# Score matmuls in row tiles: two batches issued one behind the other, with four buffers for the transposed Q and K

## The chip, the cores and the metric

The kernel runs on one core of a Trainium2 chip. The metric is the device time of one execution in microseconds (us). Every number is of executions that were not slow, except where a slow one is the subject. The time before was 304.8 us (median of 3 runs).

The names of the engines: PE is TensorE's matmuls, PEld its weight loads, DVE VectorE, ACT ScalarE, POOL GpSimd, SPq the queue that issues transfers. "L300" is line 300 of the kernel.

## The reference, cut to what matters

Two parts follow one another: a gated linear attention, and a sum of four experts over its output.

```python
def _attn_ref(q, k, v, f_logit):            # B, H, S, D = 4, 8, 768, 48
    f = 1.0 / (1.0 + np.exp(-f_logit))
    for t in range(S):
        state = f[:, :, t, :, None] * state + np.einsum('bhd,bhe->bhde', k[:, :, t], v[:, :, t])
        y[:, :, t] = np.einsum('bhd,bhde->bhe', q[:, :, t], state)

def _moe_ref(x, domain_probs, w1, w2):      # x: 3072 x 384, 4 experts, 1024 hidden
    for e in range(E):
        h = np.maximum(x @ w1[e], 0.0)
        out += p[:, e:e + 1] * (h @ w2[e])
```

## The kernel before

The sequence is cut into six chunks of 128 positions. Within a chunk the attention is matmuls: scores (Q times K, per head), a mask, scores times V plus the carried state. A head has 48 numbers, so a score matmul contracts over 48 rows only. Two heads lie in one buffer, at rows 0 to 47 and 64 to 111, and their matmuls go to two row tiles of TensorE:

```python
    def pe_at(c, b):                         # one score block: 8 matmuls, chunk c, batch b
        QK = tl("QK", c, b)
        for i in range(NP):                  # NP = 4
            for r in range(2):
                rows = slice(r * P2, r * P2 + D)     # 48 rows, from 0 or from 64
                nc.tensor.matmul(out=tl("A", c, b, r)[:, i, :], lhsT=QK[rows, 1, i, :], rhs=QK[rows, 0, i, :],
                                 start=True, stop=True)
```

The two results of a batch, A with r = 0 and 1, are one bank each of PSUM, the memory that TensorE writes its results to, from a room of four ("ps_t": 4). VectorE multiplies each with the mask and frees it (L304). Then come the y matmuls (L311, L315), and for the next chunk the state (kv, L321).

All this is spread among the expert matmuls of the chunk before (L344 with the first weights, L356 with the second). A planner in the kernel decides the order: each step has a cost, a priority, what it waits for and which buffers it takes, and a list scheduler runs through them at build time. The chip then executes the order that came out, each engine its own list.

```python
    rooms = {"ps_m": 4, "ps_t": 4, ..., "QK": 2, "AT": 2, ...}
    ...
            at = P.add(f"at {c}.{b}", {"PE": 0.35}, on(pe_at), s(7), deps=[et],
                       takes=[pt_("A", 0), pt_("A", 1)], lag=0.2, frees=[("QK", c, b)])
```

## Time and profile before

| | |
|---|---|
| span in the profile | 302.7 us |
| TensorE busy | 97% |
| next busiest engine, ScalarE | 56% |
| score matmuls (L300) | 192, in 24 blocks of 8 |
| first expert matmul starts | 22.74 us |
| from there to the end | 279.96 us |

How to read it: TensorE is the only engine that counts, and from the first expert matmul on it is hardly ever idle. What shortens its list of work shortens the kernel. The lines themselves are shown in the prediction.

The first expert matmul waits for the first expert weights to land. Span minus that start leaves this out. As the span is read to 0.1 us, such a difference is good to 0.05 us.

### The profile page before, as it was taken

How to read it: one execution, taken by the hardware profiler on the slowest of the kernel's cores; microseconds unless marked ns; L12 is line 12 of the kernel's file. 1: busy time of each engine (PE TensorE's matmuls, PEld its weight loads, DVE VectorE, ACT ScalarE, POOL GpSimd, SP SyncE). 2: the span in 40 equal slices, each digit the busy share in tenths (PEclk: the TensorE clock that was granted, in tenths of full speed). 3: DMA queues.
4: the chain of work that ended last, by engine and by line, in shares of the span. 5: the costliest groups of instructions: out<-in, count | busy, mean ns of one | idle time of the engine just before them, and what ended most of it. 6: DMA issues, size and time to landing. Idle time of an engine off the chain costs nothing.

```text
span 302.7 us, 5517 instructions
## 1 busy us (share of the span) xinstructions
PE 293.2 (97%) x2112; PEld 169.4 (56%) x2143; DVE 138.1 (46%) x273; ACT 170.8 (56%) x295; POOL 95.5 (32%) x157
## 2 busy tenths in 40 slices
PE   7899999999999999999999999999999999999995
PEld 5565555567775655455555555555555555555553
DVE  6774013787853764516555344544423443201223
ACT  5767654857865444676356475345566344475440
POOL 4584400409656237423426143522332100000000
PEclk9999999999999999999999999999999999999999
DMA  7999999954994589866997877301322201100003
GB/s 157 203 193 204 207 206 193 228 83 91 217 207 84 111 161 187 189 122 120 182 187 134 216 142 147 56 13 28 100 61 51 48 14 30 67 22 2 0 0 106
DMA packets 137355, 36.10 MB, mean 119 GB/s; under 512 B 128496, under 2 KB 135792, under 8 KB 137328
## 3 DMA queue, kind: packets, MB, share of 16 engines
q1 hardware_dynamic: 131568, 29.45, 49.1%
q0 software_dynamic: 5760, 6.29, 12.4%
q8 instruction: 17, 0.28, 0.4%
q14 instruction: 10, 0.08, 0.1%
HBM read 31.51 MB, written 4.72 MB: 120 GB/s over the span
## 4 chain that ended last, share of the span: by engine, by line
PE 88%; DMA 4%; DVE 2%; SPq 2%; issue 1%; POOL 1%; ACT 1%; DVEq 0%; ACTq 0%; POOLq 0%
PE ps_m L356 41%; PE ps_m L344 40%; DMA w_sb<-in_moe_w_dram 3%; PE ps_t L300 2%; SPq L222 2%; DMA f<-in_f_logit_dram 1%; PE ps_t L315 1%; PE ps_t L321 1%; PE ps_t L311 1%; PE ps_t L255 1%; PE ps_t L285 1%; DVE qk L276 1%; POOL qk L276 0%; DVE AT L304 0%; POOL Sf L335 0%
## 5 line engine op out<-in xcount | busy, mean ns | idle before, releaser
L352 ACT ACTIVATE h<-ps_m 128x512 bf16<-128x512 f32 (+1 forms) x171 | 98.3, 577 | 103.0 <-PE ps_m L344 92.9
L356 PE MATMUL ps_m<-w_sb,h 128*128 128x384 bf16 x776 | 153.0, 324 | 0.2
L344 PE MATMUL ps_m<-xT,w_sb 128*128 128x512 bf16 (+1 forms) x593 | 150.4, 362 | 2.1 <-DVE o L367 0.3
L356 PEld LDWEIGHTS <-h 128*128 128x128 bf16 x776 | 73.0, 98 | 57.0
L363 DVE SCALAR_TENSOR_TENSOR o<-ps_m,pn,o 128x384 f32<-128x384 f32 (+1 forms) x73 | 44.6, 611 | 96.8 <-PE ps_m L356 89.4
L344 PEld LDWEIGHTS <-w_sb 128*128 128x128 bf16 x624 | 59.8, 98 | 47.1 <-issue 0.7
L276 POOL TENSOR_TENSOR qk<-q,e 128x384 bf16<-128x384 f32 x19 | 22.8, 1204 | 64.9 <-ACT e L262 64.4
L304 DVE TENSOR_TENSOR AT<-ps_t,mask 128x512 bf16<-128x512 f32 x48 | 31.1, 683 | 19.2 <-PE ps_t L300 19.1
L335 POOL TENSOR_TENSOR Sf<-Sf,egs 48x192 f32<-48x192 f32 x40 | 20.4, 510 | 48.8 <-DVE Sf L328 46.8
L350 DVE TENSOR_SCALAR h<-ps_m 128x512 bf16<-128x512 f32 (+1 forms) x37 | 20.7, 572 | 22.0 <-PE ps_m L344 19.8
L276 POOL TENSOR_TENSOR qk<-k,e 128x384 bf16<-128x384 f32 x20 | 21.0, 1052 | 19.8 <-ACT e L264 12.9
L262 ACT ACTIVATE e<-ps_t 128x384 f32<-128x384 f32 x24 | 20.7, 864 | 3.7 <-PE ps_t L255 2.4
L328 DVE TENSOR_TENSOR Sf<-Sf,ps_t 48x192 f32<-48x192 f32 x40 | 14.0, 349 | 6.1 <-PE ps_t L321 5.3
L336 POOL CAST sb<-Sf 48x192 bf16<-48x192 f32 x40 | 13.6, 339 | 2.6
L365 ACT ACTIVATE o<-ps_m,pn 128x384 f32<-128x384 f32 x20 | 11.6, 580 | 3.9 <-PE ps_m L356 3.1
L264 ACT ACTIVATE e<-ps_t 128x384 f32<-128x384 f32 x24 | 13.0, 541 | 0.0
L556 PE MATMUL ps_m<-busy 128*128 128x256 bf16 x71 | 11.5, 301 | 1.3 <-DVE busy L140 1.3
L218 DVE CAST yb<-ps_t 128x384 bf16<-128x384 f32 x16 | 8.9, 555 | 7.4 <-PE ps_t L315 6.3
L247 ACT ACTIVATE ex<-f 128x768 f32<-128x768 f32 (+1 forms) x14 | 10.5, 748 | 3.1 <-DMA f<-in_f_logit_dram 2.9
L315 PE MATMUL ps_t<-vb,AT 128*128 128x48 bf16 x192 | 11.4, 184 | 0.7 <-DVE vb L218 0.7
L315 PEld LDWEIGHTS <-AT 128*128 128x128 bf16 x192 | 9.8, 97 | 3.0 <-issue 1.0
L251 ACT ACTIVATE gp<-ex 128x768 bf16<-128x768 f32 (+1 forms) x14 | 10.5, 751 | 0.4
(50 smaller groups left out, 139.9 us busy)
## 6 DMA issues: line engine op xcount, KB each, us to landing
w_sb<-in_moe_w_dram POOLq DMA_DIRECT2D x8, 768.0 KB, 18.8
out_dram<-o SPq DMA_DIRECT2D x23, 192.0 KB, 2.1
f<-in_f_logit_dram SPq DMA_DIRECT2D x10, 384.0 KB, 4.3
k<-in_k_dram SPq DMA_DIRECT2D x10, 384.0 KB, 5.2
q<-in_q_dram SPq DMA_DIRECT2D x10, 384.0 KB, 5.3
v<-in_v_dram SPq DMA_DIRECT2D x10, 384.0 KB, 5.5
f<-in_f_logit_dram SPq DMA_DIRECT2D x4, 192.0 KB, 4.0
k<-in_k_dram SPq DMA_DIRECT2D x4, 192.0 KB, 4.0
```

What stands on the lines that cost most here:

```text
L262: nc.scalar.activation(out=e[:, 0].rearrange("t (d h) -> t h d", d=D), in_=cs[:, 0:HD].rearrange("t (i r d) -> t r i d", r=2, d=D), func=A ...
L276: engines[eng].tensor_tensor(out=tl("qk", c, b)[:, j, :, 0:D].rearrange("t (i r) d -> t i r d", r=2), in0=tl("qk"[j], c, b // 2)[:, hh(b), ...
L304: nc.vector.tensor_tensor(out=tl("AT", c, b)[:, r].rearrange("s i t -> s (i t)"), in0=tl("A", c, b, r).rearrange("s i t -> s (i t)"), in1= ...
L315: nc.tensor.matmul(out=y[:, h * D:(h + 1) * D], lhsT=AT[:, r, i, :], rhs=vb[:, h, :], start=(c == 0), stop=True, skip_group_check=True)
L328: nc.vector.tensor_tensor(out=Sf[rows, b], in0=Sf[rows, b], in1=KV[rows, :, r, :], op=ALU.add)
L335: nc.gpsimd.tensor_tensor(out=Sf[rows, b], in0=Sf[rows, b], in1=eg, op=ALU.mult)
L336: nc.gpsimd.tensor_copy(out=nb[rows, b, :, r * D:(r + 1) * D], in_=Sf[rows, b])
L344: nc.tensor.matmul(out=tl("hp", c, e, fc, n0)[:, n0:n1], lhsT=w1_sb[:, e, kk, fc * 128:(fc + 1) * 128], rhs=tl("xT", c)[:, kk, n0:n1], sta ...
L350: nc.vector.tensor_relu(out=dst, in_=src)
L352: nc.scalar.activation(out=dst, in_=src, func=AF.Relu)
L356: nc.tensor.matmul(out=tl("op", c, e, nt, part)[:, cols], lhsT=tl("h", c, e)[:, fc, nt * T:(nt + 1) * T], rhs=w2_sb[:, e, fc, cols], start ...
L363: nc.vector.scalar_tensor_tensor(out=o, in0=op, scalar=pe, in1=o, op0=ALU.mult, op1=ALU.add)
```

## The change

Its intent: fewer changes between the 48-row mode and full height. From the third chunk on (c = 2 to 5), the score blocks of batches 0 and 1, and of 2 and 3, are one step of the planner, issued back to back. For that four QK buffers are needed, and a pair takes all four ps_t banks at once. The planner's cost of a single block goes from 0.35 to 0.4; of a pair it is 0.66.

```diff
-             "vb": 7, "egs": 8, "QK": 2, "AT": 2, "yb": 2, "xT": 2, "h": 2, "o": 6}
+             "vb": 7, "egs": 8, "QK": 4, "AT": 2, "yb": 2, "xT": 2, "h": 2, "o": 6}
...
-            at = P.add(f"at {c}.{b}", {"PE": 0.35}, on(pe_at), s(7), deps=[et],
-                       takes=[pt_("A", 0), pt_("A", 1)], lag=0.2, frees=[("QK", c, b)])
+            ET[b], VB[b] = et, vb
+
+        pairs = [[b] for b in range(B)] if c < 2 else [[b, b + 1] for b in range(0, B, 2)]
+        AT_ = {}
+        for bs in pairs:
+            at = P.add(f"at {c}.{bs[-1]}", {"PE": 0.4 if len(bs) == 1 else 0.66}, lambda e, bs=bs: [pe_at(c, b) for b in bs], slot(bs[-1], 7),
+                       deps=[ET[b] for b in bs], takes=[("ps_t", "A", c, b, r) for b in bs for r in range(2)], lag=0.2,
+                       frees=[("QK", c, b) for b in bs])
...
```

More of the change, by code (lines that the diff above doesn't have):

```diff
@@ L398, in attention @@
     def attention(c, slot, gran):
-        G, X, Y, GS = {}, [], [], []
+        G, X, Y, GS, ET, VB = {}, [], [], [], {}, {}
         more = c < C - 1
@@ L437, in attention @@
                            frees=[("qk", c, b)], lag=2.2)
-            at = P.add(f"at {c}.{b}", {"PE": 0.35}, on(pe_at), s(7), deps=[et],
-                       takes=[pt_("A", 0), pt_("A", 1)], lag=0.2, frees=[("QK", c, b)])
+            ET[b], VB[b] = et, vb
[5 more added lines that the diff above has]
+                       frees=[("QK", c, b) for b in bs])
+            for b in bs:
+                AT_[b] = at
+        for b in range(B):
+            s = lambda k: slot(b, k)
+            pt_ = lambda kind, *x: ("ps_t", kind, c, b) + x
+            on = lambda f, *x: (lambda e, b=b: f(c, b, *x))
+            at, vb = AT_[b], VB[b]
             eA = [P.add(f"ev_at{r} {c}.{b}", {"DVE": 0.7}, on(ev_at, r), s(7) + 0.1 + 0.1 * r, deps=[at],
```

## The prediction

> **What bounds the kernel now.** I read the page from the top: busy times, the chain that ended last, the costliest groups; then the waits of TensorE after the start-up, its timeline around the score matmuls, and those matmuls alone.
>
> ```profile
> PE 293.2 (97%) x2112; PEld 169.4 (56%) x2143; DVE 138.1 (46%) x273; ACT 170.8 (56%) x295; POOL 95.5 (32%) x157
> ...
> PE 88%; DMA 4%; DVE 2%; SPq 2%; issue 1%; POOL 1%; ACT 1%; DVEq 0%; ACTq 0%; POOLq 0%
> ...
> L356 PE MATMUL ps_m<-w_sb,h 128*128 128x384 bf16 x776 | 153.0, 324 | 0.2
> L344 PE MATMUL ps_m<-xT,w_sb 128*128 128x512 bf16 (+1 forms) x593 | 150.4, 362 | 2.1 <-DVE o L367 0.3
> ```
>
> TensorE is the bound: 97% busy, 88% of the chain. No other engine is over 56%. The two expert matmuls (lines 344 and 356) are nearly all of it. Busy on this engine is not work at its peak, so I go by the distance between starts. The waits from 20 us to the end show that almost nothing holds TensorE up, except one thing:
>
> ```profile
> PE ps_m L344 <- DVE o L367: 0.3, 1, 0.3
> PE ps_t L285 <- DVE qk L276: 0.3, 1, 0.3
> PE ps_m L344 <- DMA w_sb<-in_moe_w_dram: 0.3, 1, 0.3
> ...
> PEld L300 <- issue: 5.8, 15, 0.4
> ```
>
> The weight loads of line 300, the score matmuls, begin 15 times after a pause of about 0.4 us for which no semaphore is named. The timeline shows what a score block costs (columns: start, length, engine, line, operation, count):
>
> ```profile
> 106.91 0.81 PE L356 MATMUL ps_m<-w_sb,h 128*128 128x384 bf16 x4
> 107.65 0.40 PE L300 MATMUL ps_t<-QK 48*128 48x128 bf16 x8
> 107.98 0.82 PE L344 MATMUL ps_m<-xT,w_sb 128*128 128x512 bf16 x3
> 108.64 0.81 PE L356 MATMUL ps_m<-w_sb,h 128*128 128x384 bf16 x4
> 109.39 0.40 PE L300 MATMUL ps_t<-QK 48*128 48x128 bf16 x8
> 109.72 0.82 PE L344 MATMUL ps_m<-xT,w_sb 128*128 128x512 bf16 x3
> ```
>
> An expert block (four of 384 columns, or three of 512) lasts 0.65 us from start to start. From 106.91 to 107.98 are 1.07 us: 0.65 of the expert block, so 0.42 of the score block. I took the same difference at most of the blocks of chunks 2 to 5 (97.15, 109.39, 132.23, 142.66, 173.76, 196.41, 220.00, 242.25) and it was 0.42 or 0.43 each time. It divides into 0.74-0.65=0.09 before the first score matmul and 0.33 after it. How much of the 0.33 is matmul, the starts tell. This is the view of line 300 in four windows from 97.0 to 97.20, 97.26, 97.32 and 97.40; the count is what has started:
>
> ```profile
> L300 PE MATMUL ps_t<-QK x2: 226/226/226, 97.2 to 97.2; 48*128 48x128 bf16 x2
> L300 PE MATMUL ps_t<-QK x4: 216/221/226, 97.2 to 97.2; 48*128 48x128 bf16 x4
> L300 PE MATMUL ps_t<-QK x6: 216/216/226, 97.2 to 97.3; 48*128 48x128 bf16 x6
> L300 PE MATMUL ps_t<-QK x8: 216/216/226, 97.2 to 97.3; 48*128 48x128 bf16 x8
> ```
>
> They start in twos, one for each row tile, every 0.06 us. So the eight are worth 4 x 0.06 = 0.24 us, and 0.42-0.24 = **0.18 us per block is the price of entering and leaving**.
>
> **What the Trainium skill says.** (1) "TensorEngine Tiling (Array Packing)", section Key Properties: "Changing tiling mode (not just tile) drains the TensorE". The trace agrees in kind: about 0.09 us on either side of each 48-row block, with no engine named as the releaser. It is not the semaphore: in the instruction order the block at 97.15 waits for its transfer alone while most others wait for earlier matmuls too, and all cost the same. (2) "TensorE: Matmul & The Clock Gate", Part 3 on packing small matmuls: matmuls in different row groups run at the same time, with starts within about 4 ns. The trace agrees: two starts lie too close for a step of 10 ns to part them well, then 0.06 us pass. (3) "Perfetto Trace Analysis", Tensor Engine Instruction: the end of a matmul is estimated from its size, not observed. That is why I use starts only; the rows give each score matmul 216 ns, though two of them start every 60. (4) "TensorEngine Tiling", PSUM Bottleneck: row tiling does not speed up the emptying of PSUM. Here the four evictions of a pair are 4 x 0.68 us on VectorE (the group of line 304 has 683 ns), and this is where a loss would come from.
>
> **The change part by part.** *Removed:* chunks 2 to 5 have 4 batches each, 16 score blocks; they become 8 blocks of 16 matmuls. The second eight follow in the same tiling mode, so each join saves one entry and one exit: 0.18 us. 8 x 0.18 = 1.44 us. *Moved, by chance:* the instruction order of the changed kernel shows that in chunk 1 the score blocks of batches 0 and 1, which had one expert block between them, now stand next to each other (four QK buffers, and a changed cost in the kernel's own planner). One more join: 0.18. Sum **1.62 us**. *Added:* nothing on TensorE; all other matmuls keep their numbers, except that two of the 71 filler matmuls (line 556) of the first 22 us go. That stretch ends with the landing of the first expert weights (the first line 344 matmul, at 22.7 us, waits for that transfer), so they are worth nothing. The two extra QK buffers are memory only. On VectorE and ScalarE the same evictions are shared out a little differently; VectorE loses four instructions out of some 275.
>
> *What of it is on the path.* All of it, as from 85 us on TensorE waits for no engine in the list of waits (only 0.3 us for a transposed QK, once). I counted expert blocks in the order of both kernels to see whether a join moves something later that others need. The pair stands within one block of where the second of its batches stood before: (2.0, 2.1; chunk and batch) after 120 blocks instead of 115 and 119, (3.2, 3.3) after 186 instead of 175 and 185, (5.2, 5.3) after 313 instead of 303 and 313. The last y of a chunk is in the same place or one block later (134 against 133, 193, 257, 321), and the first expert matmul of the next chunk is at the same count (202, 264, 328), in chunk 2 one block earlier (141 against 142). So the work that feeds the next chunk keeps its place, and the saving reaches the end.
>
> **The rivals.** *(a) The burst of evictions makes TensorE wait.* A pair takes all four small PSUM buffers at once and leaves 2.6 to 2.7 us of VectorE work. Evictions began 0.43 to 0.64 us after the score block in the old trace (97.15 to 97.58; 107.65 to 108.29). So the first batch's are done about 1.7 to 2.4 us after the pair starts, the second's after 3.0 to 3.7. The first y stands 4 blocks behind the pair: 0.66+4x0.65 = 3.3 us. The second is at 4.1 us or later (y 0.39, kv 0.2, at times a block more). Both fit, the second with 0.4 us or more to spare. Where a VectorE instruction of another kind (0.62 us) gets in between, some 0.2 us could be lost; over 8 pairs at the worst 1.6, which would eat the gain: 304.8. I think it unlikely, since the order was planned with durations like those measured.
> *(b) A transfer comes too late.* A pair waits for the later of two transposed QKs. Its issue-to-landing time was 3.0 to 4.8 us, and the tightest block before, 4.3, came 4.9 us after its issue at 191.5; the pair comes no sooner. At chunk 2 the distance from the last y to the first expert matmul shrinks from 6.6 to 5.3 us (two blocks); transposing xT needs about 2.5 us to be issued behind its predecessor and 2.3 to land, so 4.8. If it lands in 4.1 us as others did, 1.3 us are lost there: 304.5.
> *(c) Joining saves less,* because part of the 0.18 belongs to the change of weights between batches and not to the mode: at 0.09 per join 0.8 us: 304.0.
>
> **How the range follows.** The sum gives 304.8-1.6 = 303.2. I add 0.1 for small waits under (a) and (b): **303.3 us**. Below: with every join at 0.24 and a lucky run, some 302.5. Above: (b) or half of (a), with a run-to-run spread of 1 us before (304.63 to 305.67): 304.5. A change of 2% would be 6.1 us, more than all the score blocks of the kernel together cost beyond their matmuls (24 x 0.18 = 4.3), so faster by over 2% has 0.01; slower by over 2% would need many new waits, 0.01; within 2%, 0.98.
>
> **What would show it.** In the profile of the changed kernel: score blocks of x16 in chunks 2 to 5 taking 0.66 us (0.42+0.24) instead of 2 x 0.42; the weight loads of line 300 paused without a releaser about 6 to 9 times fewer, 2.5 to 3.5 us in place of 5.8; line 344 and 356 blocks still 0.65 us apart; TensorE's waits from 85 us still near 0; a span of about 301.1 in place of 302.7. It would be wrong if a pair took 0.8 us (the drain is not what costs), if new waits of line 315 for AT or of line 300 for ps_t appear, or if line 344 waits for xT near 115 to 120 us.

## The result, and the profile after

The changed kernel took **303.65 us** (median of 6 runs, 302.98 to 304.46) against 305.0 us. The ratio is 0.9956, with a 95% interval of 0.9936 to 0.9976. A ratio here is the mean time of one kernel's fast runs over that of the other's in the same rounds, so it is not quite the ratio of the two medians. It is 1.35 us by the medians: within 2%, as forecast, and real. The page after, its busy times, its chain and the two expert groups:

```profile
PE 294.6 (97%) x2141; PEld 170.9 (56%) x2141; DVE 136.8 (45%) x269; ACT 172.1 (57%) x299; POOL 95.7 (32%) x157
...
PE 90%; DMA 4%; DVE 3%; POOL 1%; ACT 1%; issue 1%; DVEq 0%; ACTq 0%; POOLq 0%
...
L344 PE MATMUL ps_m<-xT,w_sb 128*128 128x512 bf16 (+1 forms) x624 | 153.1, 363 | 1.3 <-DMA w_sb<-in_moe_w_dram 0.9
L356 PE MATMUL ps_m<-w_sb,h 128*128 128x384 bf16 x776 | 153.2, 324 | 0.0
```

TensorE is still the bound and its busy time even rose. That is no contradiction: this trace has 2141 matmul records where the one before had 2112 (L344 had 593 of its 624), and their ends are modelled. Only starts tell. A joined block of batches 2 and 3 in chunk 2, in the timeline (start, length, engine, line, operation, count):

```profile
108.67 0.81 PE L344 MATMUL ps_m<-xT,w_sb 128*128 128x512 bf16 x3
109.41 0.62 PE L300 MATMUL ps_t<-QK 48*128 48x128 bf16 x16
109.97 0.82 PE L356 MATMUL ps_m<-w_sb,h 128*128 128x384 bf16 x4
110.63 0.59 PE L344 MATMUL ps_m<-xT,w_sb 128*128 128x512 bf16 x2
```

From 108.67 to 110.63 are 1.96 us. An expert block is 0.649 us (in the old trace eight of them lie between 124.84 and 130.03), two are 1.30, so sixteen score matmuls cost **0.66 us**. The same sum for a single block before (107.65, shown above) is 0.74+0.33+0.66-1.30 = 0.43 to 0.44. A join therefore saves 2 x 0.435-0.66 = **0.21 us**, and all eight blocks of x16 look like this one (0.74 or 0.75 before, 0.55 or 0.56 after). 8 x 0.21 = 1.68 us.

The waits from 20 us to the end:

```profile
PE ps_m L344 <- DMA w_sb<-in_moe_w_dram: 0.9, 1, 0.9
PE ps_m L344 <- DVE o L367: 0.3, 1, 0.3
PE ps_t L285 <- DVE qk L276: 0.3, 1, 0.3
...
PEld L300 <- issue: 3.9, 10, 0.4
...
PEld L285 <- DVE qk L276: 1.0, 2, 0.6
```

The pauses of the score weight loads without a releaser fell from 15 to 10. No wait of L315 or of L300 for a PSUM bank has come in, so the four evictions in a row hurt nothing. Two things are new: the first weights landed later (a wait of 0.9 in place of 0.3), and the transposes of L285 wait for a qk product twice. A third new thing hides behind a wait of L344 for "issue" and is shown below.

The span of this trace is 302.5 us, only 0.2 below. Its first expert matmul starts at 23.83 us, 1.09 later than in the trace before. From there to the end it is 278.67 against 279.96 us: **1.29 us saved**, 0.4 less than eight joins are worth. Where the rest went, chunk 1 shows. Before:

```profile
70.12 0.65 PE L285 MATMUL ps_t<-ident,qk 128*112 128x128 bf16 x8 [0.29 <-DVE qk L276]
70.61 1.80 PE L344 MATMUL ps_m<-xT,w_sb 128*128 128x256 bf16 x15
72.34 0.40 PE L300 MATMUL ps_t<-QK 48*128 48x128 bf16 x8
72.67 0.65 PE L285 MATMUL ps_t<-ident,qk 128*112 128x128 bf16 x8
```

and after:

```profile
71.68 1.47 PE L344 MATMUL ps_m<-xT,w_sb 128*128 128x256 bf16 x12
73.26 0.43 PE L285 MATMUL ps_t<-ident,qk 128*112 128x128 bf16 x4
73.62 0.40 PE L300 MATMUL ps_t<-QK 48*128 48x128 bf16 x8
73.95 0.50 PE L344 MATMUL ps_m<-xT,w_sb 128*128 128x256 bf16 x3
74.29 0.39 PE L285 MATMUL ps_t<-ident,qk 128*112 128x128 bf16 x4
```

The planner has moved the first half of the last batch's transposes ahead of a score block and of one expert block. Fifteen matmuls of 256 columns took 72.34-70.61 = 1.73 us, the 0.10 of the mode change included, so 0.109 each; twelve end at about 72.99. But the transposes start at 73.26: they came too soon for their product and TensorE stands still for **0.27 us**. The distance from chunk 1's first score block to its last grew from 75.27-59.91 = 15.36 us to 76.62-60.97 = 15.65.

One more pause, of 0.19 us, lies before L344 at 163.15 (the expert block ahead of it starts at 162.31). The profile names no engine for it, but its views show what ended it: these matmuls are the first of chunk 3's expert part and need its last transposed y (xT), a transfer (of L293: issue at 157.8, and the time to landing).

```profile
L293 SPq DMA_TRANSPOSE xT<-yb x1: 2161/2161/2161, 157.8 to 157.8; - x1
DMA to landing us min/median/max: 5.3/5.3/5.3
163.15 1.45 PE L344 MATMUL ps_m<-xT,w_sb 128*128 128x512 bf16 x6
```

157.8+5.3 = 163.1, and the trace has TensorE's queue waiting for that transfer's semaphore until 163.09. In the kernel before, the same transfer was issued at 157.07 and landed 2.3 us later, 3.1 us before its matmul (162.48).

The account: 1.68 saved by the joins, 0.29 lost in chunk 1, and 0.19 lost to the late xT. This leaves about 1.2, near the 1.29 found.

### The profile page after: what moved, and what is told of

Read it like the earlier page. It is cut to its first block, busy times and chain, and to the rows that moved or that the text cites. A ratio compares the mean times of both kernels' runs of the same rounds, so it can differ in the third digit from the quotient of the medians.

```text
span 302.5 us, 5544 instructions
## 1 busy us (share of the span) xinstructions
PE 294.6 (97%) x2141; PEld 170.9 (56%) x2141; DVE 136.8 (45%) x269; ACT 172.1 (57%) x299; POOL 95.7 (32%) x157
## 4 chain that ended last, share of the span: by engine, by line
PE 90%; DMA 4%; DVE 3%; POOL 1%; ACT 1%; issue 1%; DVEq 0%; ACTq 0%; POOLq 0%
PE ps_m L356 40%; PE ps_m L344 40%; DMA w_sb<-in_moe_w_dram 3%; PE ps_t L300 2%; PE ps_t L255 1%; PE ps_t L315 1%; PE ps_t L321 1%; PE ps_t L311 1%; POOL qk L276 1%; DMA f<-in_f_logit_dram 1%; DVE qk L276 1%; PE ps_m L569 1%; PE ps_t L285 1%; DVE AT L304 0%; POOL Sf L335 0%
## 5 line engine op out<-in xcount | busy, mean ns | idle before, releaser
L344 PE MATMUL ps_m<-xT,w_sb 128*128 128x512 bf16 (+1 forms) x624 | 153.1, 363 | 1.3 <-DMA w_sb<-in_moe_w_dram 0.9
L352 ACT ACTIVATE h<-ps_m 128x512 bf16<-128x512 f32 (+1 forms) x169 | 97.3, 577 | 98.0 <-PE ps_m L344 93.8
L344 PEld LDWEIGHTS <-w_sb 128*128 128x128 bf16 x624 | 59.5, 98 | 47.7 <-DMA w_sb<-in_moe_w_dram 1.1
L276 POOL TENSOR_TENSOR qk<-q,e 128x384 bf16<-128x384 f32 x18 | 21.6, 1204 | 64.3 <-ACT e L262 63.9
L350 DVE TENSOR_SCALAR h<-ps_m 128x512 bf16<-128x512 f32 (+1 forms) x39 | 21.9, 578 | 27.1 <-PE ps_m L344 24.2
L304 DVE TENSOR_TENSOR AT<-ps_t,mask 128x512 bf16<-128x512 f32 x48 | 30.2, 682 | 7.4 <-PE ps_t L300 7.4
L276 POOL TENSOR_TENSOR qk<-k,e 128x384 bf16<-128x384 f32 x21 | 22.2, 1059 | 20.2 <-ACT e L264 12.9
L569 PE MATMUL ps_m<-busy 128*128 128x256 bf16 x69 | 12.8, 333 | 1.3 <-DVE busy L140 1.3
L218 POOL CAST vb<-v 128x384 bf16<-128x384 f32 x18 | 9.7, 558 | 11.9 <-DMA v<-in_v_dram 9.7
L315 PE MATMUL ps_t<-vb,AT 128*128 128x48 bf16 x192 | 11.4, 184 | 0.7 <-DVE vb L218 0.7
L315 PEld LDWEIGHTS <-AT 128*128 128x128 bf16 x192 | 9.8, 97 | 2.5 <-issue 0.9
L251 ACT ACTIVATE gp<-ex 128x768 bf16<-128x768 f32 (+1 forms) x14 | 10.5, 751 | 0.4
```

The source lines that it names most:

```text
L276: engines[eng].tensor_tensor(out=tl("qk", c, b)[:, j, :, 0:D].rearrange("t (i r) d -> t i r d", r=2), in0=tl("qk"[j], c, b // 2)[:, hh(b), ...
L304: nc.vector.tensor_tensor(out=tl("AT", c, b)[:, r].rearrange("s i t -> s (i t)"), in0=tl("A", c, b, r).rearrange("s i t -> s (i t)"), in1= ...
L315: nc.tensor.matmul(out=y[:, h * D:(h + 1) * D], lhsT=AT[:, r, i, :], rhs=vb[:, h, :], start=(c == 0), stop=True, skip_group_check=True)
L344: nc.tensor.matmul(out=tl("hp", c, e, fc, n0)[:, n0:n1], lhsT=w1_sb[:, e, kk, fc * 128:(fc + 1) * 128], rhs=tl("xT", c)[:, kk, n0:n1], sta ...
L350: nc.vector.tensor_relu(out=dst, in_=src)
L352: nc.scalar.activation(out=dst, in_=src, func=AF.Relu)
```

## The experiments

Eleven more runs. In this list, "to the end" is the span less the start of the first expert matmul, each kernel in its own trace.

| run | first expert matmul, us | to the end, us | ratio of fast runs (95% interval) |
|---|---|---|---|
| before | 22.74 | 279.96 | 1 |
| changed kernel | 23.83 | 278.67 | 0.9956 (0.9936 to 0.9976) |
| after_again | 23.24 | 278.46 | 0.9936 (0.9920 to 0.9952) |
| after_third | 23.98 | 278.52 | no use, see below |
| rooms_only | 23.54 | 279.96 | 1.0001 (0.9982 to 1.0020) |
| old_cost | 22.99 | 278.21 | 0.9933 (0.9919 to 0.9948) |
| old_cost_again | 23.27 | 278.83 | 0.9941 (0.9921 to 0.9961) |
| pairs_c1 | 23.44 | 278.76 | 0.9957 (0.9942 to 0.9972) |
| pair_c1_first | slow trace | slow trace | 0.9939 (0.9915 to 0.9963) |
| split | 23.41 | 283.39 | 1.0112 (1.0078 to 1.0147) |
| wide_single | 22.77 | 280.63 | 0.9994 (0.9959 to 1.0030) |
| wide_pair | 23.37 | 280.83 | 1.0011 (0.9977 to 1.0046) |
| one_tile | 23.39 | 283.41 | 1.0096 (1.0060 to 1.0132) |

Theory A: a change into and out of the 48-row mode costs 0.2 us, the joins save just that, and chunk 1 gives a little back. Its rivals are named with each run.

### Is the late start of the changed kernel's own making? (after_again, after_third)

No edit: the changed kernel twice more.

> The changed kernel once more, unedited, for a tighter ratio and a second trace. Theory A (8 joins save 0.19 us each = 1.5 us, a new wait in chunk 1 gives back 0.26, the landing of the first expert weights scatters by chance): ratio 0.9945 to 0.9965, and the first expert matmul starts anywhere between 22.5 and 24 us in the trace. Rival B (the changed order at the start makes the first weights land about 1 us later every time, and something unseen makes up for it): the first expert matmul at 23.6 us or later again.

> The changed kernel a third time, on the same chip as the two above: ratio 0.9935 to 0.9960, 278.4 to 278.7 us from the first expert matmul to the end, so 0.2 to 0.5 us behind the version with the old cost.

The first expert matmul started at 23.24 and 23.98 us. In kernels that keep the old order to the end of the start-up it was 22.74 to 23.54 us. VectorE, ScalarE and GpSimd have the same instructions in the same order there in both kernels, and in the traces that are not slow the first weights were issued between 14.4 and 15.2 us and took 7.5 to 8.9 us to land. So the 1.09 us between the two first traces is mostly chance. Rival B in its full form fell with the 23.24 (it asked for 23.6 or later). A shift of some 0.4 us could hide in the scatter: the kernels with the new single-block cost average 23.57 (five traces), the others 23.16 (seven). That stays open. The ratio, 0.9936, is below the expected 0.9945 to 0.9965, a miss, though its interval overlaps that of the first call.

In after_third half the runs were slow. One that counts as fast took 306.68 us, and the kernel before was up to 306.31; the ratio, 1.0003 with an interval from 0.9948 to 1.0058, says nothing. Its trace, 278.52 us to the end, lies where it was expected.

### Buffers alone (rooms_only)

```diff
-"QK": 2,
+"QK": 4,
```

> The kernel before with four QK buffers in place of two and nothing else; all score blocks single. Theory A: buffers alone are worth nothing on TensorE; 16 blocks in chunks 2 to 5 still cost 0.42 us each; ratio 0.999 to 1.001. Rival E (part of the gain is from the earlier issue of the QK transposes, not from the joins): ratio 0.997 or lower.

The ratio was 1.0001, and to the end 279.96 us, as before. Rival E is out: the buffers make the pairing possible and do nothing by themselves.

### The planner's cost of a single block (old_cost, old_cost_again)

```diff
-{"PE": 0.4 if len(bs) == 1 else 0.66}
+{"PE": 0.35 if len(bs) == 1 else 0.66}
```

> The change with one number put back: the planner's cost of a single score block is 0.35 as before, not 0.4. The pairs from chunk 2 on stay; in chunk 1 the order of TensorE is that of the kernel before again (in the instruction order). Theory A: the 0.26 us lost in chunk 1 come back, ratio about 0.995 (gain 1.5 us), TensorE waits for a qk product once for 0.3 us, and the distance from the first expert matmul to the score block of batch 3 of chunk 1 is that of before (52.5 us) and not 52.8. Rival C (the 0.26 comes from elsewhere): the distance stays 52.8 and the ratio is that of the changed kernel.

> The version with the old planner cost once more, as a second sample beside the run above: ratio 0.992 to 0.9945 again, 278.2 us from the first expert matmul to the end, and the first expert matmul anywhere between 22.7 and 23.9.

The distance from chunk 1's first score block to its last was 15.34 and 15.35 us, as before (15.36; rooms_only 15.36), against 15.65, 15.64 and 15.65 in the three traces of the changed kernel. The second wait for a qk product was gone, in the waits of the first run:

```profile
PEld L285 <- DVE qk L276: 0.6, 1, 0.6
```

So the loss of 0.29 us in chunk 1 comes from the changed cost of single blocks, through the planner's order, and not from the pairs. Rival C of this run is out. The expectation named another distance, from the first expert matmul to chunk 1's last score block: it was 52.5 us, as expected, in the first run, but 52.8 in the repeat, since a pause at 54.9 us lies in it. The ratio, 0.9933, is a larger gain than the 0.995 expected.

A second miss: the repeat took 278.83 us to the end where 278.2 had been expected. It had two pauses of 0.3 us, at 54.9 and 162.7 us, that the first run of the same program did not have. At 54.9 the profile names ScalarE (L251, the gate), and the step before it there had waited for a load of f; wide_single and wide_pair below have this pause too (0.4 us). At 162.7 it is the late xT again: issued at 157.4, landed 5.2 us later. In all five traces of the changed kernel and old_cost this transfer took 4.7 to 5.3 us; in the other three the matmul started 0.1 to 0.7 us after the landing and lost nothing. In the kernel before and in rooms_only it took 2.3 us. Why it took twice that is not shown: the transpose ahead of it is issued 1.9 to 2.9 us earlier here and 7.5 there, but in pairs_c1 that distance is 1.9 us too, and it landed in 2.3. So a few tenths in "to the end" must not be built on.

By time, this version (0.9933, 0.9941) and the changed kernel (0.9956, 0.9936) overlap. It is the better one by the trace of chunk 1, and the runs don't separate them.

### The same again, one chunk earlier (pairs_c1, pair_c1_first)

The first on the changed kernel, the second on old_cost:

```diff
-... if c < 2 else [[b, b + 1] for b in range(0, B, 2)]
+... if c < 1 else [[b, b + 1] for b in range(0, B, 2)]                                   # pairs_c1
+... if c < 1 else [[0, 1], [2], [3]] if c == 1 else [[b, b + 1] for b in range(0, B, 2)]  # pair_c1_first
```

> The change taken one chunk further: pairs from chunk 1 on, ten in all. Theory A: two more joins, 0.38 us, if no new waits appear: ratio about 0.9943 (gain 1.7 us). Rival D: chunk 1 still transposes on TensorE and needs ScalarE or VectorE for every step, so a pair there has no room; new waits of 0.5 to 2 us in chunk 1 eat the two joins: ratio 0.995 to 1.000.

> The version with the old planner cost, and one more pair: batches 0 and 1 of chunk 1, which stood two expert blocks apart; its batches 2 and 3 stay single. Theory A: one more join of 0.21 us if no wait is added: from the first expert matmul to the end 278.0 us in place of 278.2, ratio 0.9926. Rival D: the delay of the first batch by two blocks puts its chain (y, transpose, xT) behind, and the wait costs more than 0.2: ratio 0.9935 or higher.

Both of chunk 1's pairs together gained nothing: ratio 0.9957, and TensorE's waits between 60 and 100 us are new:

```profile
PE ps_m L344 <- DVE o L367: 1.1, 1, 1.1
PE ps_m L344 <- ACT h L352: 0.8, 1, 0.8
```

In chunk 1 the transposed QK is evicted by ScalarE or VectorE, and four score evictions at once come on top; the expert matmuls then wait for their own PSUM banks. That the evictions are the reason is argued from the order, not tested. Two joins (0.42 us) were bought with 1.9 us of waits, of which 0.3 to 0.4 (L367) was there already; the waits of L285 for a qk product (0.3 each) are gone in exchange. Rival D was right here. The single pair came out at 0.9939, which does not separate it from old_cost (0.9941). By the expectation's numbers this is rival D's side (0.9935 or higher), but the interval holds theory A's 0.9926 too. Its trace fell in the slow state and can't be compared; but it shows what a slow run of this program is. ScalarE, in the timeline:

```profile
17.57 1.01 ACT L216 COPY QK<-ps_t 112x1024 bf16<-112x1024 bf16 x1 [0.64 <-PE ps_t L285]
28.44 0.51 ACT L216 CAST vb<-v 128x384 bf16<-128x384 f32 x1 [9.86 <-DMA v<-in_v_dram]
```

The cast of a V tile of chunk 0 waited 9.9 us for its load, while the expert weights were being loaded too, and TensorE stood still for 8.4 us behind it. In this trace the lower mean clock (0.984) goes with that idle stretch in the start-up: the clock was 0.63 from 20 to 30 us and 1.00 from 40 us on. The first expert matmul came at 32.83 us, and from there to the end were 278.1 us, so the whole loss lies before it.

### Doubling the suspected cost (split)

The kernel before, chunks 2 to 5 only, with a first and second half of each block as steps of their own:

```diff
+                a1 = P.add(f"at1 {c}.{b}", {"PE": 0.3}, on(pe_at, 0, 2), s(7), deps=[et],
+                           takes=[pt_("A", 0), pt_("A", 1)], lag=0.5)
+                at = P.add(f"at2 {c}.{b}", {"PE": 0.3}, on(pe_at, 2, 4), s(7), deps=[a1],
+                           lag=0.2, frees=[("QK", c, b)])
```

> The opposite of the change, on the kernel before: in chunks 2 to 5 each score block of 8 is cut into two of 4 with other TensorE work between them, so 32 blocks in place of 16. Theory A (each entry and exit of the 48-row mode costs about 0.2 us, and nothing else is tied to the number of blocks): 16 more, so 3.2 to 3.5 us longer, ratio 1.010 to 1.012; blocks of x4 take about 0.32 us each. Rival C of the prediction (part of the price belongs to the batch, not to the block): less than 2 us, ratio below 1.007.

```profile
97.06 0.81 PE L344 MATMUL ps_m<-xT,w_sb 128*128 128x512 bf16 x3
97.80 0.29 PE L300 MATMUL ps_t<-QK 48*128 48x128 bf16 x4
98.02 0.82 PE L356 MATMUL ps_m<-w_sb,h 128*128 128x384 bf16 x4
98.78 0.28 PE L300 MATMUL ps_t<-QK 48*128 48x128 bf16 x4
...
PEld L300 <- issue: 12.2, 33, 0.4
```

Half a block takes 0.74-0.65+0.22 = 0.31 us, not half of 0.43. To the end it is 3.43 us longer, 3.43/16 = **0.21 us for each additional block**, the same as a join saves. The pauses went from 15 to 33. So the price belongs to the block, not to the batch; rival (c) of the prediction is out.

### No row tiling at all (wide_single, wide_pair)

In chunks 2 to 5 each score matmul takes all 112 rows and so sums two heads. Their outputs are wrong, which doesn't matter for the times. Counts, order and waits are those of the kernel before and of the changed one.

```diff
-                rows = slice(r * P2, r * P2 + D)
+                rows = slice(r * P2, r * P2 + D) if c < 2 else slice(0, MP)
```

> Wrong result on purpose. The kernel before, but in chunks 2 to 5 the score matmuls take all 112 rows of QK (both heads summed) in place of the 48 rows of a tile: same count, same order, same waits, no row tiling. Theory A: no pause before or after the block; 8 x 0.056 = 0.45 us a block against 0.43, so ratio 0.999 to 1.002, and the pause of the line 300 weight loads without a releaser is left in chunks 0 and 1 only (about 1.5 us in place of 5.8). Rival F (the pause comes from the semaphores or the new PSUM banks, not from the tiling): block 0.45+0.2 = 0.65 us, 3.5 us longer, ratio 1.011.

> Wrong result on purpose. The changed kernel with the same 112-row score matmuls in chunks 2 to 5, so joined but without row tiling. Theory A: joining is worth nothing here, 16 x 0.056 = 0.89 us a pair against 2 x 0.45 single; same time as wide_single but for the 0.26 us of chunk 1: ratio 1.000 to 1.003. Rival F: 1.5 us or more faster than wide_single.

wide_single, timeline and waits:

```profile
107.29 0.81 PE L356 MATMUL ps_m<-w_sb,h 128*128 128x384 bf16 x4
107.94 0.61 PE L300 MATMUL ps_t<-QK 112*128 112x128 bf16 x8
108.39 0.81 PE L344 MATMUL ps_m<-xT,w_sb 128*128 128x512 bf16 x3
...
PEld L300 <- issue: 0.6, 2, 0.3
```

The score matmuls now start 0.65 us after the expert block, right in step, and the expert block behind them 0.45 us later: 0.056 us each, and no pause. Joined (wide_pair) they take 0.89 us, so a join is worth nothing: 280.83 us to the end against 280.63, and the 0.29 of chunk 1 is in it. Both have the late gate at 54.5 and 55.0 us (0.4 us), which is about half of what they are behind the kernel before. Rival F (semaphores or PSUM banks make the pause) is out: the waits are the same and the pause is gone.

### The mode without the second tile (one_tile)

In chunks 2 to 5 all eight take rows 0 to 47. Its output is wrong, which doesn't matter for the time.

```diff
-                rows = slice(r * P2, r * P2 + D)
+                rows = slice(r * P2, r * P2 + D) if c < 2 else slice(0, D)
```

> Wrong result on purpose. The kernel before, but in chunks 2 to 5 all eight score matmuls take rows 0 to 47, so the 48-row mode stays and the second row tile is not used. Theory A with the mode as the cause: the pause on either side stays (0.09 before the block) and the eight follow each other at 0.056 us in place of two at a time: 0.45+0.2 = 0.65 us a block, 3.5 us longer in all, ratio 1.011. Rival G (the pause comes from working two tiles at once): no pause, 0.45 us a block, ratio 1.000 to 1.002.

```profile
107.95 0.81 PE L356 MATMUL ps_m<-w_sb,h 128*128 128x384 bf16 x4
108.70 0.62 PE L300 MATMUL ps_t<-QK 48*128 48x128 bf16 x8
109.25 0.82 PE L344 MATMUL ps_m<-xT,w_sb 128*128 128x512 bf16 x3
```

The pause of about 0.1 us before the block (0.75 for a 0.65 block) is there again, and the eight follow one another: 0.55 us to the next start against 0.33. Beside wide_single (0.65 and 0.45) the same eight matmuls cost 0.1 us more on either side, 0.20 in all. 3.45 us longer to the end. Rival G is out: it is the change between 48 rows and full height that costs, not the work on two tiles at once.

## Why the prediction was right

- **The bound and the path** were right: TensorE's list of work sets the end, and from 85 us on the changed kernel's TensorE still waits for no engine that the profile names. It does wait once for a transfer that the list of waits doesn't name, 0.19 us at 163.15. "The work that feeds the next chunk keeps its place" was thus too strong: counted in expert blocks it does, but the 3.1 us that chunk 3's last xT had to spare shrank to 0.7 or less.
- **The price of a block** was right in kind and slightly small: 0.18 predicted, 0.21 measured two ways (the joins and the doubled blocks), with 0.20 between one_tile and wide_single. Two terms were off: the second eight cost 0.66-0.435 = 0.23 us and not 0.24, and I had cut the old block off at 0.42, though the expert block behind it also starts its successor 0.01 late. The eight joins are thus 1.68 us in place of 1.44.
- **The step that failed** is "Moved, by chance": the two score blocks of chunk 1 were not joined. They had two expert blocks between them before and have one now (60.97, L344 at 61.30, 62.05 in the trace); the instruction order says the same and I misread it. In its place stands a move that I had seen and not weighed: the transposes of the last batch of chunk 1, half of them moved ahead of their product. That costs 0.29 us where 0.18 was to be gained. The larger joins (0.24 more) and this loss nearly cancel, which is luck: 1.62-0.18+0.24-0.29 = 1.39, beside 1.35 by the medians.
- **Rival (a)**, evictions in a row, did not come about in chunks 2 to 5: no wait of y or of the score blocks for VectorE or a bank. It did in chunk 1 when pairs were tried there.
- **Rival (b)**, a transfer that comes too late: not before chunk 2's first expert matmul, where it was feared (no such wait in any of the three traces), but before chunk 3's. There the last xT landed late in one of the three traces (0.19 us) and in the repeat of old_cost (0.3 us).
- **Rival (c)**, that part of the price belongs to the batch: refuted by the doubled blocks.
- **The signs**: x16 blocks at 0.66 us as said. The pauses were to be 6 to 9 fewer, between 2.5 and 3.5 us in all: they were 5, 6 and 5 fewer, at 3.9, 3.5 and 3.9 us. The span was to be 301.1 and was 302.5, 301.7 and 302.5, as the first weights landed late by chance in the first and the third trace.

## What to carry to other kernels

In this kernel matmuls that work in another tiling mode than their neighbours had a price for each visit, 0.21 us for 4, 8 and 16 matmuls alike, so issue them in as few runs as the buffers allow; for short runs ask whether tiling pays at all (eight in two row tiles, alone among full-height work, took 0.43 us, and at full height 0.45, though that version summed two heads and would need operands that give the right result). A pair is free only where its evictions find an idle engine: in chunks 2 to 5 they did, in chunk 1 they apparently did not. Look also at the transfers behind it: a wait for "issue" can be a transfer that lands late, so compare its landing with the start of what needs it. Where a planner orders the steps, read its whole new order, as an edit to one cost moved work in a part that the change was not about.

## What the Trainium skill lacked or had wrong

- "TensorEngine Tiling (Array Packing)", Key Properties, says that changing the mode drains TensorE, without a size. Here entering and leaving together cost 0.21 us, about 0.1 of it before the first tiled matmul, and one row tile alone paid it as well (3.45 us for 16 blocks, which includes the lost overlap of the two tiles).
- The same page's table of speedups gives two row tiles up to 2x and no break-even. Eight matmuls of 128 columns in two row tiles took 0.43 us against 0.45 at full height; sixteen took 0.66 against 0.89.
- "TensorE: Matmul & The Clock Gate", Back-to-back issue gap, gives some 131 ns for 512 columns and 81 ns for 128 in a stream with a weight load for each matmul. Here three of 512 took 0.65 us, 216 ns each, and eight of 128 with a weight load each took 0.45 us, 56 ns each. These are the figures that the same section gives for the isolated gap (about 216 and 56 ns) and says to be off in such a stream.
- No page that I read describes what the slow state of a one-core program can be. In the one slow trace here it was a load that landed late in the start-up: ScalarE waited 9.9 us for it, TensorE 8.4.
